# Recurrence and soft mixture of experts on one core: more unread matmuls around the first units, one gate in two halves, constants copied earlier, slot inputs in another PSUM bank

## The chip, the cores and the metric

The kernel runs on one core of one Trainium2 chip. The metric is device time in microseconds (us) of one execution; the time of a kernel is the median of its runs. The core has five instruction streams that run beside each other: TensorE (PE, with its weight loads as PEld), VectorE (DVE), ScalarE (ACT), GpSimd (POOL) and SyncE (SP, which here only issues transfers), and 16 transfer (DMA) engines that all queues share. TensorE writes to PSUM, which VectorE and ScalarE read; the other working memory is SBUF.

## The reference

Two layers follow each other. With x and f_logit of shape (4, 5056, 256), the first is a recurrence over the sequence, in each of the 4 sequences and 256 channels:

```python
f = lower_bound + (1.0 - lower_bound) * sigmoid(f_logit)
for t in range(S):
    h = f[:, t] * h + (1.0 - f[:, t]) * x[:, t]
    y[:, t] = h
```

The second is a soft mixture of experts over all N = 20224 tokens, with 8 experts of 4 slots each (32 slots) and a hidden width of 1024:

```python
logits = x @ phi                                   # N x 32
d = softmax of logits over the tokens              # to the slots
slot_input = d.T @ x                               # 32 x 256
slot_out[e] = relu(slot_input[e] @ w1[e]) @ w2[e]  # per expert
c = softmax of logits over the slots               # back to the tokens
return c @ slot_out                                # N x 256
```

The slots need every token, so no row of the output can be made before the whole input has been read.

## The kernel before, in words

**Units.** The 5056 tokens of a sequence are cut into 10 groups of 512 (the last two are shorter or overlap). One group of one sequence is a *unit*: 40 units, numbered 0 to 39. Units 0 to 3 are loaded one at a time; from unit 4 on (`long`) two neighbouring groups of one sequence are loaded as a pair, 1 MB of f_logit and 1 MB of x, by SyncE (`load`, lines 207 to 224). The tiles of the loads have three buffers each, so a load waits until the gate (f_logit) or the product (x) of the pair three before it is done.

**What one unit goes through**, each step on its own engine:

- `gate` (226): ScalarE takes the sigmoid of -f_logit, which gives s = 1 - sigmoid. It works on one unit (k=1) or on a pair (k=2, the default).
- `enter` (236): GpSimd multiplies s by x and gives u (unit 0: VectorE).
- `s_to_channels` (266) and `u_to_channels` (275): TensorE transposes s and u to put channels on partitions. Units 0 to 3 take four 128x128 transposes; a long unit takes, for u, eight half transposes (`half_to_channels`, 260), the first four from the u of the pair's even unit and the last four from that of the odd one. So a long unit's u needs the products of both units of its pair.
- `decay` (288): ScalarE turns the transposed s into the factor of the recurrence.
- `scan` (323, instruction at line 332): VectorE runs the recurrence, two scans of 512 tokens for a unit.
- `to_tokens` (339) and `keep_tokens` (355): TensorE transposes the states back, and VectorE or ScalarE copies them out of PSUM. There is one PSUM buffer for this.
- For each two groups: `logits` (371), `exps` (383), `weights_to_tokens` (390) and `slots` (423), which adds to the slot inputs in `slot_ps`.

**Order.** The order of the instructions on each engine is written out by hand: a prologue for units 0 to 2 (lines 481 to 498), then a loop over n from 0 to 39 (499 to 595), in which step n starts the scan of unit n, the u of unit n+1, the s of units n+2 and n+3, the product of unit n+3 and the loads six units ahead. `SINGLE` is 4, so `n < SINGLE - 2` are steps 0 and 1. Each engine works off its own list in order.

**Unread matmuls.** `idle` (177) issues f32 matmuls of 128x256 whose sum nobody reads, into the second half of the bank that holds `slot_ps`; the moving operand is `wide_rep`, a view of the constant `rep`. Its first call opens that half with two small bf16 matmuls (`first=True`). The kernel before calls it first at step 2, and then at steps 9, 13, 14, 15 and so on, behind the u of unit n+1.

**Constants.** `rep` holds the 32x32 identity repeated; GpSimd copies it out of an identity in four parts, one for each sequence (`rep_constants`, 84), two in step 0 and two in step 1, each behind the product of the step (`enter`).

**Weights.** GpSimd also issues the loads of the experts' weights (`load_w`, 135), which are read as f32 and stored as bf16, at steps 9, 17, 25, 31 to 34 and 36; the last matrix comes in three parts, and the last two go into a tile `w_t` that reuses a buffer of f_logit.

**The end.** After the last unit come the slot inputs. `slot_sb` is copied out of `slot_ps`; two small products per half put channels on partitions in `sin_ps` (616), a part of the bank `tail[:, 0]`, which also takes the row sums (`row_sums`, 407; at 621 and 622 they follow directly). Lines 631 and 632 read `sin_ps`, on VectorE and on ScalarE. Then come the hidden layer (638 to 656), the second layer (681 to 706, products at 696) and `slot_out` (708). From 713 on the output: matmuls with the tokens' weights (727, 760, 801), division by the row sums on VectorE and ScalarE, and stores issued by SyncE.

Of the kernel before, what the change touches and what calls it, by code (L numbers as in the profile page):

```python
# [18 lines left out]
def kernel(  # L19
# [10 lines left out]
    nc = tc.nc  # L30
# [73 lines left out]
    def lb_constants():  # L104
        row = lb_row.rearrange("u (p o) -> u p o", o=DC)
        lb_ps = ptp.tile([P, R, P], F32, name="lb_ps", tag="tp")
        lb = lb_ps[:, 0, ds(0, DC)]
        for o in range(DC):
            nc.tensor.transpose(lb_ps[:, 0, ds(o, 1)], row[:, :, o], ident_f[ds(0, 1), ds(0, 1)])
        nc.vector.tensor_scalar(omlb, lb, -1.0, 1.0, ALU.mult, ALU.add)  # L110
        nc.vector.tensor_scalar(nomlb, lb, 1.0, -1.0, ALU.mult, ALU.add)
# [50 lines left out]
    with tc.tile_pool(name="sp2", bufs=3) as sp2, \  # L162
# [11 lines left out]

        wide_rep = rep.rearrange("p b s -> p (b s)").unsqueeze(1).broadcast_to([P, 2, P])

        def idle(k, first=False):
            if first:
                for i in range(2):
                    nc.tensor.matmul(slot_bank[:, 1, ds(0, P)], ident, ident,  # L180
                                     start=True, stop=False, skip_group_check=True)
            for _ in range(k):
                nc.tensor.matmul(slot_bank[:, 1], ident_f, wide_rep,  # L183
                                 start=False, stop=False, skip_group_check=True)
        xs, fs, sts, uts, pss, psus, hs, hps, hts, lgs, ets = ({} for _ in range(11))

# [39 lines left out]
        def gate(n, k=2):  # L226
            if n % 2 == 0:
                sts[n // 2] = sp2.tile([P, 2, R, D], BF16, name="s_t", tag="s_t")
            s_t, f_t = sts[n // 2][:, ds(n % 2, k)], fs[n // 2][:, ds(n % 2, k)]
            if n // B == odd:  # L230
                m = R7 * D
                s_t = s_t.rearrange("p u r d -> p (u r d)")[:, :m]
                f_t = f_t.rearrange("p u r d -> p (u r d)")[:, :m]
            nc.scalar.activation(s_t, f_t, ACT.Sigmoid, scale=-1.0)  # L234
# [22 lines left out]
                nc.tensor.matmul(v[:, :, :, r], t(r)[k].bitcast(F32), sides,  # L257
                                 is_transpose=True, start=True, stop=True)

        def half_to_channels(n, ps, t):  # L260
            k = ds(n % 2 * (P // 2), P // 2)
            v = ps.rearrange("c p r -> c (p r)").rearrange("c (p r) -> c p r", r=2 * R)
            for r in range(2 * R):
                nc.tensor.transpose(v[:, :, r], t(r)[k].bitcast(F32), ident_f[k, k])  # L264

        def s_to_channels(n):
            if n % 2 == 0:
                pss[n // 2] = psp.tile([P, 2, P, R], F32, name="sp", tag="sp")
            ps = pss[n // 2][:, n % 2]
            if n // B == odd:  # L270
                woven_to_channels(n, ps, lambda r: sts[n // 2][:, r // R, r % R])
            else:
                to_channels(n, ps, sts[n // 2][:, n % 2])

        def u_to_channels(n):
            ps = psu.tile([P, P, R], F32, name="up", tag="up")
            if long(n):
                half_to_channels(n, ps, lambda r: uts[n - n % 2 + r // R][:, r % R])
            elif n // B == odd:
                woven_to_channels(n, ps, lambda r: uts[n - n % 2 + r // R][:, r % R])  # L280
            else:
                to_channels(n, ps, uts[n])
            psus[n] = ps.rearrange("c p r -> c (p r)").bitcast(BF16).rearrange(
                "c (t o) -> c t o", o=DC)
# [149 lines left out]
        def unit(f, m):  # L434
            if 0 <= m < n_unit:
                f(m)
# [45 lines left out]
            load(n, 1)  # L482
        load(SINGLE)
        lb_constants()
        gate(0, 1)
        enter(0)
        s_to_channels(0)
        decay(0, 1, [0])
        u_to_channels(0)
        gate(1, 1)  # L490
        decay(0, 1, [1])
        phi_constants()
        enter(1)
        s_to_channels(1)
        u_to_channels(1)
        gate(2, 1)
        decay(1, 1)
        enter(2)
        for n in range(n_unit):
            if n < SINGLE - 2:  # L500
                if n:
                    unit(to_tokens, n - 1)
                    unit(u_to_channels, n + 1)
                s_to_channels(n + 2)
                if n + 3 < SINGLE:
                    gate(n + 3, 1)
                decay(n + 2, 1)
                if n + 3 == SINGLE:
                    gate(n + 3)
                if n % 2 == 0:  # L510
                    unit(load, n + AHEAD)
                unit(enter, n + 3)
                for b in range(2 * n, 2 * n + 2):
                    rep_constants(b)
            else:
                end = n >= n_unit - 6
                if n % 2 == 0:
                    unit(load, n + AHEAD)
                    if n == SINGLE - 2:
                        to_tokens(n - 1)  # L520
                        keep_tokens(n - 1)
                    if not end and n >= SETTLED:
                        unit(gate, n + 4)
                else:
                    unit(decay, n + 1)
                    if n in (late + 1, late + 3):
                        keep_tokens(n - 2)
                    if n < SETTLED:
                        gate(n + 3)
                    if n == n_unit - 5:  # L530
                        gate(n + 3)
                        exps(odd - 1)
                if not end and n != n_unit - 7:
                    group(exps, n - 2)

                unit(enter, n + 3)
                for _ in range(W_AT.get(n, 0)):
                    load_w(w_next[0])
                    w_next[0] += 1

                if n in (n_unit - 3, n_unit - 2):
                    unit(u_to_channels, n + 1)
                if n in (late, late + 2):
                    to_tokens(n - 2)
                elif n not in (SINGLE - 2, late - 1, late + 1):
                    unit(to_tokens, n - 1)
                if n == n_unit - 2:
                    keep_tokens(n - 1)
                if n % 2 == 0:
                    unit(s_to_channels, n + 2)  # L550
                    unit(s_to_channels, n + 3)
                if n not in (n_unit - 3, n_unit - 2):
                    unit(u_to_channels, n + 1)
                if n in (n_unit - 5, n_unit - 4):
                    idle(2)
                elif n == SINGLE - 2:
                    idle(1, True)
                elif 2 * B <= n < n_unit - 4 and n % (2 * B) in (1, 5, 6, 7):
                    idle(1)
                if n == n_unit - 2:  # L560
                    tail = psp.tile([P, 2, G], F32, name="tail", tag="sp")
                    sums = tail[:, 0]
                    rs_ps = sums[:, ds(0, n_grp * R * B)].rearrange(
                        "p (q b) -> p q b", b=B)
                    late_ps, odd_ps = (
                        tail[:, 1].bitcast(BF16)[:, ds(i * R * P, R * P)].rearrange(
                            "p (r s) -> p r s", r=R) for i in range(2))
                    logits(odd)
                    exps(odd)
                    slots(odd - 2)  # L570
                elif not end and by_pairs(n - 1):
                    if n % B == 0:
                        g = (n - 1) // (2 * B) * 2
                        for i in range(2):
                            logits(g + i, [2, 3] if n % (2 * B) == 0 else [0, 1])
                elif not end:
                    group(logits, n - 1)
            if n == n_unit - 1:
                odd_weights()
                logits(last, [0, 1, 2])  # L580

            unit(scan, n)
            if n in (late, late + 2):
                keep_tokens(n - 2)
                to_tokens(n - 1)
            elif n not in (SINGLE - 2, late - 1, late + 1, n_unit - 2):
                unit(keep_tokens, n - 1)
            if n == n_unit - 3:
                weights_to_tokens(odd - 1, nc.scalar.copy)
            elif not n >= n_unit - 6:  # L590
                group(weights_to_tokens, n - 3)
                batch(slots, n - 4, 0)
                batch(slots, n - 4, 1)
                if n > 2 * B and n % (2 * B) == 3:
                    idle(1)
# [17 lines left out]
        slot_sb = hpool.tile([P, G, DC], BF16, name="slot_sb", tag="h")  # L613
        slot_sb = slot_sb.rearrange("p t o -> p (t o)").bitcast(F32)[:, ds(0, D)]
        nc.vector.tensor_copy(slot_sb, slot_ps)
        sin_ps = tail[:, 0, ds(G // 2, DC * NS)].rearrange("p (o s) -> p o s", o=DC)
        slot_v = slot_sb.rearrange("p (c o) -> p o c", o=DC)
        for o in range(DC):
            nc.tensor.matmul(sin_ps[:, o], slot_v[:, o], rep[:, 0],
# [250 lines left out]
```

## Time and profile before

| what | value |
|---|---|
| time, median of 3 runs | 197.94 us (197.11, 197.94, 198.4) |
| the profiled execution | 197.01 us, its span 195.2 us |
| mean granted TensorE clock | 0.845 |
| PE busy, share of the span | 150.6 us, 77% |
| DVE | 142.0 us, 73% |
| ACT | 138.8 us, 71% |
| POOL | 103.1 us, 53% |
| read from HBM, written to it | 58.23 MB, 20.71 MB |

The span runs from the first to the last instruction of the profiled execution; 1.8 us of its time lie outside. Times in a view are counted from the start of the span. The page gives busy time by engine, the span in 40 slices, the chain of waits that ended last and the costliest groups of instructions; the trace behind it also answers with a timeline of any stretch and with tables of stretches. A group's line reads: line of the kernel, engine, operation, output<-inputs, shapes, count | busy us, mean ns of one | idle time of the engine just before them, and what ended it:

```profile
L245 POOL TENSOR_TENSOR u_t<-s_t,x_t 128x1024 bf16<-128x1024 bf16 (+1 forms) x39 | 82.4, 2129 | 24.5 <-ACT s_t L234 14.2
L332 DVE TENSOR_TENSOR_SCAN h<-a,h,up 128x512 bf16<-128x512 f32 x64 | 78.1, 1267 | 9.0 <-PE up L264 4.3
...
L183 PE MATMUL slot_ps<-rep,ident_f 128*128 128x256 f32 x42 | 14.2, 426 | 0.0
```

The product of one unit takes GpSimd 2.13 us and one scan takes VectorE 1.27 us, two for a unit; the 21 unread matmuls show as 42 records, two for each f32 matmul. Busy time on TensorE is modelled, since its matmuls overlap.

### The profile page before, as it was taken

Reading aid. Unit: us, or ns where it says so; the run is one execution under the profiler, and the core shown is the slowest. Engines: PE = TensorE matmul, PEld = TensorE weight load, DVE = VectorE, ACT = ScalarE, POOL = GpSimd, SP = SyncE. Lnnn points to the kernel's source line nnn. Section 1 sums busy time; section 2 is a strip of 40 time slices with the busy share of each in tenths; the row PEclk is TensorE's granted clock in tenths of the full one; section 3 lists DMA queues with packets and bytes.
Section 4 is the critical chain, followed back from the end, with each engine's and each line's share of the span. In section 5 each row is a group of like instructions: output and inputs, shape, how many; then the busy total and the mean of one; then the engine's idle time right before and its main releaser. Section 6 shows DMA issues by size and latency. Waiting matters only on the chain.

```text
span 195.2 us, 3283 instructions
## 1 busy us (share of the span) xinstructions
PE 150.6 (77%) x1222; PEld 108.7 (56%) x1222; DVE 142.0 (73%) x175; ACT 138.8 (71%) x192; POOL 103.1 (53%) x78
## 2 busy tenths in 40 slices
PE   0684896898998979989798976999997999980000
PEld 0474775765786657857576755766872663420000
DVE  2666699799699999999999999824288867770000
ACT  3686778599988998989988698724068788991000
POOL 2584888756798949776888979592030000000000
PEclk9998799699699999999999999999985555555555
DMA  6999999999999999999999999999949999999995
GB/s 203 415 433 428 426 425 421 430 426 411 326 428 426 423 334 405 423 425 414 324 418 418 235 212 214 214 212 211 170 165 428 425 431 426 430 433 430 430 430 218
DMA packets 12145, 70.75 MB, mean 362 GB/s; under 512 B 1361, under 2 KB 1874, under 8 KB 7650
## 3 DMA queue, kind: packets, MB, share of 16 engines
q1 hardware_dynamic: 9504, 62.13, 76.3%
q0 software_dynamic: 2624, 8.42, 21.8%
q8 instruction: 9, 0.15, 0.3%
q14 instruction: 6, 0.05, 0.1%
q10 hardware_dynamic: 2, 0.00, 0.0%
HBM read 58.23 MB, written 20.71 MB: 404 GB/s over the span
## 4 chain that ended last, share of the span: by engine, by line
PE 36%; DVE 28%; DMA 17%; ACT 4%; issue 4%; SPq 1%; POOL 0%; ACTq 0%
DVE h L332 17%; DMA w_t<-in_moe_w_dram 7%; PE op L801 7%; PE sp L249 7%; PE op L727 6%; DMA w_sb<-in_moe_w_dram 6%; PE hp L345 5%; DVE ht L364 5%; PE up L264 4%; DMA f_t<-in_f_logit_dram 4%; DVE h L319 3%; DVE oc L717 2%; PE op L760 2%; ACT s_t L234 1%; PE lg L378 1%
## 5 line engine op out<-in xcount | busy, mean ns | idle before, releaser
L245 POOL TENSOR_TENSOR u_t<-s_t,x_t 128x1024 bf16<-128x1024 bf16 (+1 forms) x39 | 82.4, 2129 | 24.5 <-ACT s_t L234 14.2
L332 DVE TENSOR_TENSOR_SCAN h<-a,h,up 128x512 bf16<-128x512 f32 x64 | 78.1, 1267 | 9.0 <-PE up L264 4.3
L234 ACT ACTIVATE s_t<-f_t 128x2048 bf16<-128x2048 f32 (+2 forms) x22 | 38.1, 1736 | 2.9 <-DMA f_t<-in_f_logit_dram 2.9
L345 PE MATMUL hp<-ident_f,h 128*128 128x128 f32 (+1 forms) x160 | 29.3, 307 | 8.4 <-DVE ht L364 6.3
L297 ACT ACTIVATE a<-sp,lbs 128x1024 f32<-128x1024 bf16 x28 | 29.6, 1112 | 4.6 <-PE sp L249 4.5
L345 PEld LDWEIGHTS hp<-ident_f,h 128*128 128x128 f32 (+1 forms) x160 | 23.2, 206 | 17.0 <-DVE ht L364 11.5
L249 PE MATMUL sp<-ident_f,s_t 128*128 128x128 f32 x144 | 23.7, 315 | 7.0 <-ACT s_t L234 5.7
L249 PEld LDWEIGHTS sp<-ident_f,s_t 128*128 128x128 f32 x144 | 19.6, 164 | 8.7 <-ACT s_t L234 6.5
L264 PE MATMUL up<-ident_f,u_t 64*128 64x64 f32 x224 | 21.4, 236 | 2.4 <-POOL u_t L245 2.4
L264 PEld LDWEIGHTS up<-ident_f,u_t 64*128 64x128 f32 x224 | 17.0, 144 | 7.1 <-POOL u_t L245 2.8
L721 ACT ACTIVATE ob<-op,rrow 128x256 f32<-128x256 f32 x32 | 12.4, 478 | 9.1 <-PE op L727 8.7
L364 ACT COPY ht<-hp 128x512 f32<-128x512 f32 (+1 forms) x21 | 12.2, 583 | 7.9 <-PE hp L345 7.9
L304 ACT ACTIVATE a<-sp,lbs 128x512 f32<-128x512 bf16 (+2 forms) x16 | 13.2, 868 | 2.9 <-PE sp L249 2.7
L183 PE MATMUL slot_ps<-rep,ident_f 128*128 128x256 f32 x42 | 14.2, 426 | 0.0
L364 DVE COPY ht<-hp 128x512 f32<-128x512 f32 (+1 forms) x19 | 12.7, 668 | 1.0 <-PE hp L345 1.0
L801 PE MATMUL op<-slot_bd,etall 64*128 64x512 bf16 x32 | 13.1, 627 | 0.0
L812 ACT ACTIVATE oc<-op,rrow 128x256 f32<-128x256 f32 x32 | 12.2, 486 | 0.8 <-PE op L801 0.3
L727 PE MATMUL op<-slot_out,etall 32*128 32x256 bf16 x64 | 12.6, 375 | 0.1
L806 DVE TENSOR_TENSOR oc<-op,rrow 128x1024 f32<-128x1024 f32 x8 | 9.7, 1223 | 3.4 <-PE op L801 3.4
L717 DVE TENSOR_TENSOR ob<-op,rrow 128x1024 f32<-128x1024 f32 (+2 forms) x12 | 9.8, 862 | 2.2 <-DMA out_dram<-ob 1.1
L727 PEld LDWEIGHTS <-etall 32*128 32x128 bf16 x64 | 8.9, 153 | 3.8 <-issue 1.3
L378 PE MATMUL lg<-h,phi 128*32 128x512 bf16 (+1 forms) x80 | 9.9, 389 | 0.2 <-ACT et L402 0.2
(109 smaller groups left out, 168.9 us busy)
## 6 DMA issues: line engine op xcount, KB each, us to landing
f_t<-in_f_logit_dram SPq DMA_DIRECT2D x14, 1024.0 KB, 11.2
x_t<-in_x_dram SPq DMA_DIRECT2D x14, 1024.0 KB, 9.5
out_dram<-oc SPq DMA_DIRECT2D x4, 2048.0 KB, 13.1
w_sb<-in_moe_w_dram POOLq DMA_DIRECT2D x14, 512.0 KB, 9.5
out_dram<-ob SPq DMA_DIRECT2D x3, 2048.0 KB, 9.6
f_t<-in_f_logit_dram SPq DMA_DIRECT2D x8, 512.0 KB, 7.0
x_t<-in_x_dram SPq DMA_DIRECT2D x8, 512.0 KB, 6.1
out_dram<-oc SPq DMA_DIRECT2D x4, 896.0 KB, 6.0
```

The lines of the kernel that those rows point to most:

```text
L183: nc.tensor.matmul(slot_bank[:, 1], ident_f, wide_rep, start=False, stop=False, skip_group_check=True)
L234: nc.scalar.activation(s_t, f_t, ACT.Sigmoid, scale=-1.0)
L245: nc.gpsimd.tensor_tensor(uts[n][:, :r], s_t[:, :r], x_t[:, :r], ALU.mult)
L249: nc.tensor.transpose(ps[:, :, r], t[:, r].bitcast(F32), ident_f)
L264: nc.tensor.transpose(v[:, :, r], t(r)[k].bitcast(F32), ident_f[k, k])
L297: nc.scalar.activation(a, sp[:, :, :, :, o], ACT.Identity, scale=nomlb[:, ds(o, 1)], bias=1.0)
L332: nc.vector.tensor_tensor_scan(h[:, :T, o], decays[n // 2, o][:, n % 2, :T], up[:, :T, o], hs[number(g - 1, b)][:, ds(used(g - 1) - 1, 1), ...
L345: nc.tensor.transpose(hp[:n_p, r], hw[:, :n_p, r], ident_f)
L364: copy(hts[g][:n_p, b].rearrange("p r d -> p (r d)").bitcast(F32), hps.pop(n)[:n_p].rearrange("p r c -> p (r c)"))
L717: nc.vector.tensor_tensor(ob, op, scale.broadcast_to(list(ob.shape)), ALU.mult)
L727: nc.tensor.matmul(op[:, j], ew[:, :, r + j], slot_out[ds(b * NS, NS)], start=True, stop=True, skip_group_check=True)
L801: nc.tensor.matmul(op[:, i_r].rearrange("p u d -> p (u d)"), ew[:, :, r + i_r], slot_bd[ds(j * 2 * NS, 2 * NS)].rearrange("s u d -> s (u d)"),
```

## The change

- `idle` can take another moving operand. `plain`, a view of the identity, is there from the start, while `rep` is not.
- New calls: three in front of unit 0's s (with the opening that step 2 had), two in front of unit 1's s, one in front of unit 1's u, four at step 2 in front of the s of units 4 and 5, and one each at steps 3, 5 and 7 behind the u of unit n+1; at step 11, two in the middle of unit 12's u, between its two halves. In all 15 more.
- The gate of units 4 and 5, at step 1, is issued as two instructions of one unit each.
- In step 1 the last two copies of `rep` come in front of unit 4's product on GpSimd, no longer behind it. With the two of step 0 all four now stand between the products of units 3 and 4.
- `sin_ps` moves from the bank of the row sums to the half bank that `idle` writes.

```diff
+        plain = ident_f.unsqueeze(1).broadcast_to([P, 2, P])
+
-        def idle(k, first=False):
+        def idle(k, first=False, moving=wide_rep):
             if first:
                 for i in range(2):
                     nc.tensor.matmul(slot_bank[:, 1, ds(0, P)], ident, ident,
                                      start=True, stop=False, skip_group_check=True)
             for _ in range(k):
-                nc.tensor.matmul(slot_bank[:, 1], ident_f, wide_rep,
+                nc.tensor.matmul(slot_bank[:, 1], ident_f, moving,
                                  start=False, stop=False, skip_group_check=True)
...
-        def half_to_channels(n, ps, t):
+        def half_to_channels(n, ps, t, rests=False):
...
             for r in range(2 * R):
+                if r == R and rests:
+                    idle(2)
                 nc.tensor.transpose(v[:, :, r], t(r)[k].bitcast(F32), ident_f[k, k])
...
             if long(n):
-                half_to_channels(n, ps, lambda r: uts[n - n % 2 + r // R][:, r % R])
+                half_to_channels(n, ps, lambda r: uts[n - n % 2 + r // R][:, r % R],
+                                 n == 3 * B)
...
         lb_constants()
+        idle(3, True, plain)
         gate(0, 1)
         enter(0)
         s_to_channels(0)
         decay(0, 1, [0])
         u_to_channels(0)
+        idle(2, moving=plain)
         gate(1, 1)
         decay(0, 1, [1])
         phi_constants()
         enter(1)
         s_to_channels(1)
+        idle(1, moving=plain)
         u_to_channels(1)
...
                 if n + 3 == SINGLE:
-                    gate(n + 3)
+                    gate(n + 3, 1)
+                    gate(n + 4, 1)
                 if n % 2 == 0:
                     unit(load, n + AHEAD)
-                unit(enter, n + 3)
+                if n == 0:
+                    unit(enter, n + 3)
                 for b in range(2 * n, 2 * n + 2):
                     rep_constants(b)
+                if n:
+                    unit(enter, n + 3)
...
+                if n == SINGLE - 2:
+                    idle(4, moving=plain)
                 if n % 2 == 0:
                     unit(s_to_channels, n + 2)
                     unit(s_to_channels, n + 3)
...
-                elif n == SINGLE - 2:
-                    idle(1, True)
+                elif n in (SINGLE - 2, SINGLE - 1, SINGLE + 1, SINGLE + 3):
+                    idle(1)
...
-        sin_ps = tail[:, 0, ds(G // 2, DC * NS)].rearrange("p (o s) -> p o s", o=DC)
+        sin_ps = slot_bank[:, 1, ds(0, DC * NS)].rearrange("p (o s) -> p o s", o=DC)
```

## The prediction

> **What bounds the kernel now.** I read the slices of the span first, then the chain that ended last, then the end of the input stage as a timeline, then tables of stretches. The three rows of slices (the granted TensorE clock, the busy share of the transfer engines, what they moved):
>
> ```profile
> PEclk9998799699699999999999999999985555555555
> DMA  6999999999999999999999999999949999999995
> GB/s 203 415 433 428 426 425 421 430 426 411 326 428 426 423 334 405 423 425 414 324 418 418 235 212 214 214 212 211 170 165 428 425 431 426 430 433 430 430 430 218
> ```
>
> One slice is 4.88 us. The transfer engines are full in every slice but the first, the one at 146 us and the last. From slice 22 on GB/s halves with the share unchanged: the weights are then read as f32 and stored as bf16, so 212 stored is 424 read. The page gives 58.23 MB read; at the 427 that the stretch from 10 to 20 us shows that takes 136.4 us, and the stream in fact runs from about 2.6 to 141.5 us, 138.9 us. The clock row has three dents, at slices 3-4, 7 and 10. The chain that ended last, near the end of that stream (start, length, what):
>
> ```profile
> 126.92 14.59 DMA w_t<-in_moe_w_dram
> 141.52 0.04 issue
> 141.56 0.39 PE so_ps L696 x2
> 141.95 0.02 issue
> 141.98 0.49 DVE slot_out L708
> ```
>
> The last weights were issued at 126.92, landed at 141.52 behind everything queued before them, and the output waits for them. The timeline of TensorE shows how nearly the arithmetic was late too:
>
> ```profile
> 139.50 1.79 PE L696 MATMUL so_ps<-w_t,wide 128*128 128x256 bf16 x14
> ...
> 141.56 0.38 PE L696 MATMUL so_ps<-w_t,wide 128*128 128x256 bf16 x2 [0.27 <-DMA w_t<-in_moe_w_dram]
> ```
>
> TensorE came to the last two products 0.27 us before their weights. So two chains end together: arithmetic at 141.29 and the load stream at 141.52. The change shortens only the first. Where it has room, the timeline of VectorE, which paces units 2 to 39, shows; in brackets the idle time before the group and what ended it:
>
> ```profile
> 21.44 2.46 DVE L332 TENSOR_TENSOR_SCAN h<-a,h,up 128x512 bf16<-128x512 f32 x2 [2.63 <-PE up L249]
> ...
> 39.11 2.45 DVE L332 TENSOR_TENSOR_SCAN h<-a,h,up 128x512 bf16<-128x512 f32 x2 [1.51 <-PE up L264]
> ...
> 52.80 2.45 DVE L332 TENSOR_TENSOR_SCAN h<-a,h,up 128x512 bf16<-128x512 f32 x2 [1.61 <-PE up L264]
> ```
>
> Each of the three waits lies in a dent. Stretches cut where the clock changes (length, busy time of PE, PEld, DVE, ACT, POOL with counts, clock, transfer share, GB/s):
>
> ```profile
> 15.11:18.52 3.41, 0.73 (x6) 0.54 (x5) 2.65 (x3) 3.06 (x3) 0.95 (x3) 1.00 1.00 423
> 18.52:21.94 3.42, 3.42 (x15) 3.17 (x16) 0.79 (x2) 1.42 (x2) 3.16 (x4) 0.50 1.02 434
> ...
> 32.18:35.59 3.41, 1.85 (x14) 1.49 (x15) 3.38 (x4) 3.36 (x3) 2.25 (x2) 1.00 1.01 425
> ...
> 45.83:49.24 3.41, 2.44 (x30) 1.62 (x30) 3.41 (x5) 3.38 (x3) 1.22 (x1) 1.00 1.03 390
> ...
> 69.72:73.14 3.42, 2.45 (x30) 1.65 (x30) 3.42 (x5) 3.42 (x4) 2.26 (x2) 1.00 1.04 313
> ```
>
> After a stretch of 3.41 us in which TensorE was busy for 0.73, 1.85 or 2.44 us, the next one was granted half the clock; after one of 2.45 (69.72) it was not.
>
> **The change, part by part.** *Gate in two halves.* One activation of 1.91 us becomes two of 1.06 (the row of units 0 to 3), 0.21 us more ScalarE. Unit 4's half is done at 16.56 + 1.06 = 17.62 instead of 18.47, unit 5's at 18.68; SyncE's next f_logit load, which waits for both, goes out 0.2 later into a full queue. Unit 5's four transposes then end near 19.3 at full clock (eight take 1.04 at 24.99, 1.97 at half clock), unit 3's four (0.63) at 19.95, and the scan that began at 21.44 begins near 19.97. *Constants.* Two copies (0.61 us) move ahead of unit 4's product into GpSimd's wait of 2.48 us there. Queued behind them are that product and unit 5's; unit 4's x lands at 5.61 + 12.6 = 18.2 (its issue and its time to landing), so the product starts at 18.2 in place of 18.60 and unit 5's ends at 18.2 + 2 x 2.14 = 22.5 in place of 23.64. No DMA is issued by GpSimd in this stretch; SyncE's load that waits for this product goes out a microsecond earlier, into a full queue. Unit 4's scan needs that product's transposes (0.47): 23.0 instead of 24.39. Gain on VectorE's chain 1.4 us.
>
> *Unread matmuls.* Fifteen more of 128x256 in f32, two records each; one at 55.46 let the next transpose start at 56.00, so 0.54 each. They go into TensorE's waits: 1.96 us before unit 0 (two small ones, 0.42, and three: 2.0), 1.19 before unit 1's s (two: 1.1), 0.57 before its u (one), 2.68 before unit 4 (four: 2.2, but that wait is now 0.85 shorter, so 0.3 over), 0.37, 0.61 and 0.36 before the transposes behind units 3, 5 and 7 (one each: 0.17 and 0.18 over, one hidden), 0.82 between the halves of unit 12 (two: 0.26 over). Queued behind each are the next transposes, and VectorE's scan waits for those: at most 0.9 us in all if every cover is gone. If they do keep the clock, the waits of 1.51 and 1.61 us go, 3.1 us, since the eight transposes there fall from 1.92-1.97 to 1.04. No row shows an unread matmul in these places: their worth lies between 0 (dents stay) and 3.1; I take 3.1, as the dented stretches were idle for 2.7, 1.6 and 1.0 us and the added work fills most of that.
>
> *Slot inputs in their own bank.* The two conversions of the slot input waited for the row sums that follow it in the old bank: 131.21, though its own matmuls ended at 129.85 + 0.61 = 130.46. VectorE's can start there; TensorE, behind row sums to 131.10, begins the hidden layer near 131.1 in place of 131.52. Gain 0.4.
>
> Sum for the arithmetic: 1.4 + 3.1 + 0.4 - 0.9 = 4.0 us earlier. What is late next is the stream: TensorE now waits for the last weights, and the end moves only with their landing. The stream is full and the order of its issues is the same, so a lead in arithmetic buys transfer time only where the engines were short of work. That is 106 to 112 us, where the weights begin to be issued: 195 GB/s stored in 110 to 112 (390 read), against 427, loses 0.17 us, and about as much before it. Bounds 0 and 0.4; I take 0.2. Against its own execution (197.01, span 195.2 and 1.8 around it) the sum is 196.8. The median of the three runs, 197.94, stands 0.93 above that execution. If their excess is late arithmetic (dents in other places; the slack is only 0.27 us), it goes; if it is the stream's rate, it stays. I take nearly half of it: 196.8 + 0.4 = 197.2.
>
> **The rivals.** *A: the stream sets the end* (above): 196.4 to 197.9. For it: share 1.0 throughout, loads landing 6 to 16 us after issue.
>
> *B: the dents stay or move.* Rows for: 2.44 and 2.45 us of busy time with different outcomes, so where a window is cut decides. Against: the added work raises the busy time of all three stretches. Price: no 3.1, perhaps the 0.9 of added work, less 1.4 + 0.4 gained: arithmetic still 0.9 us earlier, so nothing is lost, and part of the excess goes: 197.3 to 197.9; with the 1.4 lost as well, 0.5 us later against 0.27 of slack: 198.2. The Trainium skill ("TensorE: Matmul & The Clock Gate", Part 1, What's actually happening) says that the clock's windows run free of the kernel's start; by it every execution cuts its dents elsewhere, and the nearly equal pair of rows agrees. The same page (Why this matters for your kernels) asks for idle gaps of about 3 us before the clock falls; the trace disagrees, since the longest idle gap ahead of the dents is 2.68 us and ahead of the third 0.82.
>
> *C: slower, by the clock at the output's start.* The last full weights of the second matrix but two land at 122.51 + 14.0 = 136.5, and their eight products take 1.03: 137.5. What is left lands at 138.9, 140.2, 140.9 and 141.5 (issues plus 15.9, 16.7, 16.4, 14.6) and takes 1.8 us. So with a lead of 4 us TensorE idles for 2.2 of the last 4.0 us, where the stretch from 137.99 to 141.40 is now busy for 3.30 of 3.41; about 1.6 would be left, less than the 1.85 after which the clock was halved. The half clock then meets the last two products (0.38), and the first two matmuls of the output, and delays all the output, as the stream of stores is full behind it: +0.4 to 0.6 us; the pieces after that are paced by the conversions (0.48 each), not by TensorE. With no excess removed that is 197.94 + 0.5 = 198.5, slower than before. It decides from a lead of about 2 us on and if a window is cut there. Against: the stretch from 114.10 to 117.51, busy for 2.30 with 0.9 us of unread matmuls among it, was not followed by a dent, and the last products are matmuls of the same full width.
>
> *D: the stream itself gets faster.* Deeper queues could lift it to the 429 GB/s of the store stage's slices: 58.23 / 429 = 135.7 us, 3.2 us less, 193.8. Against: share is 1.0 already with queues 7 to 12 us deep. The Trainium skill ("DMA: Bandwidth & Descriptors", Where 436 GB/s comes from) sets the ceiling at 435 GB/s, by which 133.9 us would do, 5 us less; the trace touches 435 only in the stores, 156 to 176 us.
>
> **How the numbers follow.** A 0.66, B 0.13, C 0.13, D 0.07, and 0.01 for none of them. The time is A's, 197.2. The range takes A whole, B, and C to its price: 196.0 to 198.5; D is left out. A measurement of this kernel tells about 1%, 2 us. Faster by that (under 195.96) is D: 0.07. Slower by that (over 199.9) would be C at four times its price; of C and the unnamed I put 0.03 there. Within 1%: 0.90.
>
> **What would show it.** Clock row without dents in slices 3 to 10; the three waits of VectorE near 0; VectorE's last scan ends before 123 (now 125.6); TensorE's waits for the last weights grow from 0.27 to over 1.5 us in sum; the last weights still land between 141 and 141.6. I am wrong if they land before 140, or if TensorE again comes to the last products within 0.3 us of them.

## The result, and the profile after

| | before | after |
|---|---|---|
| time, median (runs) | 197.53 us (6, 196.81 to 198.5) | 200.05 us (6, 199.28 to 201.29) |
| the profiled execution, its span | 197.01, 195.2 us | 199.28, 197.5 us |
| instructions of TensorE in the trace | 2480 | 2540 |

Both were timed side by side. The ratio is 1.0137, with a 95% interval of 1.0093 to 1.0181: 2.5 us slower, where 197.2 us was forecast. Medians here and below are over all runs, while the ratios leave out executions that count as slow, so the two can differ. The profiled executions lie 2.27 us apart, and those can be taken to pieces. The slices of the span after (4.94 us each):

```profile
PEclk9999999699999999999999999999785555555555
DMA  6999999999999999999999999999559999999992
GB/s 211 420 433 428 426 421 425 425 428 366 369 426 426 396 346 426 426 426 332 399 414 376 236 216 211 213 212 213 86 197 433 421 438 421 418 438 448 438 425 123
```

Of the three dents in the clock row one is left, at slice 7. But where the input ends (slices 28 and 29) the transfer engines now stand at 5 tenths twice, where before one slice stood at 4. The timeline of VectorE, after (idle time before the group in brackets):

```profile
19.18 2.46 DVE L337 TENSOR_TENSOR_SCAN h<-a,h,up 128x512 bf16<-128x512 f32 x2 [0.98 <-PE up L251]
23.00 2.33 DVE L337 TENSOR_TENSOR_SCAN h<-a,up 128x512 bf16<-128x512 f32 x2 [0.78 <-PE up L268]
...
38.18 2.45 DVE L337 TENSOR_TENSOR_SCAN h<-a,h,up 128x512 bf16<-128x512 f32 x2 [1.61 <-PE up L268]
50.59 2.45 DVE L337 TENSOR_TENSOR_SCAN h<-a,h,up 128x512 bf16<-128x512 f32 x2 [0.34 <-PE up L268]
...
128.75 0.25 DVE L645 TENSOR_SCALAR sin<-slot_ps,lbs 128x32 bf16<-128x32 f32 x1 [0.86 <-PE slot_ps L633]
...
143.04 0.48 DVE L722 TENSOR_SCALAR slot_out<-so_ps,rcs 128x256 bf16<-128x256 f32 x1 [5.88 <-PE so_ps L710]
```

The arithmetic did get its lead: the slot input is converted at 128.75 instead of 131.21, 2.46 us earlier. `slot_out` nevertheless starts at 143.04, not at 141.98. The timeline of TensorE between the two:

```profile
136.39 1.03 PE L710 MATMUL so_ps<-w_sb,wide 128*128 128x256 bf16 x8
139.90 3.11 PE L710 MATMUL so_ps<-w_t,wide 128*128 128x256 bf16 x16 [2.47 <-DMA w_t<-in_moe_w_dram]
142.80 1.06 PE L152 MATMUL tail<-w_sb 128*128 128x128 bf16 x8
143.92 1.90 PE L741 MATMUL op<-slot_out,etall 32*128 32x256 bf16 x16
```

TensorE waits 2.47 us for the first part of the last weights, then runs the last 16 products in 3.11 us, because the clock was halved: the stretches of the clock say why (columns as in the tables above, the clock third from the end).

```profile
136.96:140.37 3.41, 0.94 (x10) 0.69 (x8) 0.20 (x2) 0.00 (x0) 0.00 (x0) 1.00 1.01 184
140.37:143.78 3.41, 3.41 (x22) 2.52 (x19) 0.48 (x1) 0.00 (x0) 0.07 (x1) 0.51 0.12 19
```

After a stretch with 0.94 us of work the next one ran at 0.51. (Line 152 is eight unread matmuls that both kernels have behind the products; at half clock they take 1.06 us, not 0.61, and the output's first matmul stands behind them until 143.92, though `slot_out` ended at 143.53.) The difference of the spans, stage by stage, from the starts, ends and landings in the two traces:

| stage | before | after | later by |
|---|---|---|---|
| last weights land | 141.52 | 142.28 | 0.76 |
| from there to the start of `slot_out` | 0.46 | 0.76 | 0.30 |
| end of `slot_out` to the first store's issue | 1.12 | 1.39 | 0.27 |
| first store's issue to the last landing | 50.44 | 51.38 | 0.94 |

The sum is 2.27. The 0.57 in the middle is the half clock (rival C). The first and the last row, 1.70 us, were in no case of the prediction. The table of transfer queues over the time of the stores (143 to 198 us; packets, MB, share) differs in one line. Before:

```profile
q1 hardware_dynamic: 2592, 20.71, 89.1%
q14 instruction: 1, 0.01, 0.1%
```

After:

```profile
q1 hardware_dynamic: 2592, 20.71, 89.2%
q8 instruction: 1, 0.02, 0.1%
q14 instruction: 1, 0.01, 0.0%
```

The same bytes are stored, and one packet more goes over the engines: a block of instructions. The trace's list of transfers has each of them: 16384 bytes, 0.88 to 0.98 us on one of the 16 engines, nine in the whole span before, ten after. The tenth went out at 168.47, in the middle of the stores. The ninth went out at 141.24 before, when nearly all weights had landed, and at 137.70 after, when they had not. The trace has 16 landings for each load, one for each engine as it is read here. From that point on the last of them falls behind the others (times from the list of landings, us):

| part of the last matrix | before: last landing but one, last | after: last landing but one, last |
|---|---|---|
| 1 | 138.91, 138.92 | 138.76, 139.85 |
| 2 | 140.13, 140.24 | 140.02, 141.05 |
| 3 | 140.81, 140.87 | 140.70, 141.67 |
| 4 | 141.48, 141.52 | 141.33, 142.28 |

The last landing but one is 0.11 to 0.15 us earlier than before, and one is about a microsecond behind it in all four parts. (That the late one is the same engine each time is a reading too: the list doesn't name the engine.) The end of the stores looks the same. Counted from the first store's issue, the last two landings of all come at 50.06 and 50.44 us before, and at 50.43 and 51.38 us after. That gave the theory for the experiments: **the added matmuls cost by being fetched**. The 15 of them are 60 instructions (each f32 matmul of this kernel is two weight loads and two matmuls). TensorE's fetches move forward by that much, one of them lands in front of the last weights, and one more falls among the stores. The rivals: the **lead** itself does the harm (TensorE idle, half clock, other order of transfers), or the **other edits** do.

A rule bears on this that the prediction had not weighed. The Trainium skill ("Runtime: NRT & Kernel Launch", Instruction fetch mechanics) says that instructions are refilled in 16 KiB blocks of 256 over a transfer queue of the engine's own, and that the cost of a block's boundary is mostly hidden. Block size and queue agree with the 16384-byte packets here; that they are hidden does not, with 0.94 us in the stores.

### The profile page after: what moved, and what is told of

The parts are those of the page before. It is cut to its first block, busy times and chain, and to the rows that moved or that the text cites. A ratio compares the mean times of both kernels' runs of the same rounds, so it can differ in the third digit from the quotient of the medians.

```text
span 197.5 us, 3344 instructions
## 1 busy us (share of the span) xinstructions
PE 154.7 (78%) x1252; PEld 111.3 (56%) x1252; DVE 142.3 (72%) x175; ACT 139.1 (70%) x193; POOL 103.2 (52%) x78
## 4 chain that ended last, share of the span: by engine, by line
PE 28%; DMA 21%; DVE 19%; ACT 8%; POOL 8%; issue 4%; SPq 2%; ACTq 0%; POOLq 0%
DVE h L337 12%; DMA x_t<-in_x_dram 11%; DMA w_t<-in_moe_w_dram 9%; PE op L815 7%; POOL u_t L247 6%; PE op L741 6%; PE up L268 4%; PE hp L350 3%; PE sp L251 3%; DVE ht L369 3%; DVE h L324 3%; ACT oc L781 2%; ACT s_t L236 2%; POOL w_sb L147 2%; PE so_ps L710 2%
## 5 line engine op out<-in xcount | busy, mean ns | idle before, releaser
L350 PE MATMUL hp<-ident_f,h 128*128 128x128 f32 (+1 forms) x160 | 28.5, 301 | 7.1 <-DVE ht L369 5.1
L251 PE MATMUL sp<-ident_f,s_t 128*128 128x128 f32 x144 | 20.9, 288 | 3.0 <-ACT a L309 1.4
L251 PEld LDWEIGHTS sp<-ident_f,s_t 128*128 128x128 f32 x144 | 17.4, 149 | 5.3 <-ACT s_t L236 2.8
L185 PE MATMUL slot_ps<-rep,ident_f 128*128 128x256 f32 x52 | 17.1, 419 | 0.0
L337 DVE TENSOR_TENSOR_SCAN h<-a,up 128x512 bf16<-128x512 f32 x8 | 9.4, 1210 | 1.7 <-PE up L268 0.8
```

The lines of the kernel that those rows point to most:

```text
L185: nc.tensor.matmul(slot_bank[:, 1], ident_f, moving, start=False, stop=False, skip_group_check=True)
L251: nc.tensor.transpose(ps[:, :, r], t[:, r].bitcast(F32), ident_f)
L337: nc.vector.tensor_tensor_scan(h[:, :T, o], decays[n // 2, o][:, n % 2, :T], up[:, :T, o], hs[number(g - 1, b)][:, ds(used(g - 1) - 1, 1), ...
L350: nc.tensor.transpose(hp[:n_p, r], hw[:, :n_p, r], ident_f)
```

## The experiments

The fetches and stages of all kernels, each from its profiled execution (us; instructions of TensorE as the trace records them; the stage of the stores is from the first store's issue to the last landing; the last column is the median against that of the kernel before in the same session):

| kernel | instr. | 9th fetch | 10th fetch | last weights land | stores | median |
|---|---|---|---|---|---|---|
| before | 2480 | 141.24 | none | 141.52 | 50.44 | |
| after | 2540 | 137.70 | 168.47 | 142.28 | 51.38 | +2.5 |
| e1_tail_count | 2540 | 141.60 | 178.87 | 141.74 | 51.40 | +1.0 |
| e2_no_added | 2480 | 141.38 | none | 141.62 | 50.43 | 0.0 |
| e3_no_spin | 2524 | 137.74 | 173.26 | 142.32 | 52.73 | +2.3 |
| e4_fill_wait | 2539 | 138.20 | 167.72 | 142.15 | 51.41 | +1.8 |
| e5_front_count | 2540 | 139.44 | 167.93 | 142.29 | 51.40 | +1.9 |
| e6_same_count | 2480 | 143.47 | none | 143.49 | 50.42 | +3.1 |
| e7_matmuls_only | 2540 | 138.72 | 168.17 | 142.52 | 51.42 | +2.2 |
| e8_front_20 | 2500 | 141.19 | none | 141.65 | 50.44 | +0.3 |
| e9_front_40 | 2520 | 141.86 | 173.41 | 143.56 | 51.38 | +1.9 |

The expectations of e1 to e4 count from the 197.5 us of the first six runs; in their own session the kernel before took 197.10.

**e1_tail_count: the count alone, at the end.** The kernel before, with 30 unread bf16 matmuls (60 instructions) behind TensorE's last work, where nothing waits for them:

```diff
                 couple(i, j)
+        extra = pout.tile([P, R, D], F32, name="op", tag="op")
+        for _ in range(30):
+            nc.tensor.matmul(extra[:, 0, ds(0, P)], ident, ident,
+                             start=True, stop=True, skip_group_check=True)
```

> The kernel before, with 30 unread bf16 matmuls (60 instructions) behind the last matmul of TensorE, where nothing waits for them. Instruction theory: TensorE's instructions come in transfers of 16 KB, one for some 256 of them, and each holds one of the 16 transfer engines for 0.95 us; the longer program needs a tenth one, in the middle of the stores, so the last store lands about 0.9 us later and the first store is issued when it was (143.6): 197.5 becomes 198.4. Clock theory (the half clock at the start of the output is the whole of the loss): nothing changes here, 197.5, and stores take 50.4 us from the first issue to the last landing.

Measured: 198.13 us against 197.10, ratio 1.0052 (1.0017 to 1.0087). Its queues over the stores:

```profile
q1 hardware_dynamic: 2592, 20.71, 89.2%
q8 instruction: 1, 0.02, 0.1%
q14 instruction: 1, 0.01, 0.1%
```

Up to the first store nothing moved by more than 0.23 us, and the stage of the stores takes 51.40 us, 0.96 more. Matmuls that do nothing and for which nobody waits cost the time of one fetch.

**e2_no_added: the change without the 15 matmuls.** Gate in halves, constants, slot inputs in their own bank stay.

```diff
         lb_constants()
-        idle(3, True, plain)
         gate(0, 1)
...
-                elif n in (SINGLE - 2, SINGLE - 1, SINGLE + 1, SINGLE + 3):
-                    idle(1)
+                elif n == SINGLE - 2:
+                    idle(1, True)
```

(and so at the other new calls)

> The changed kernel without the fifteen added unread matmuls: gate in halves, constants and slot inputs stay as changed. The program is as long as before. Instruction theory: nine transfers of instructions, none in the stores, and the last weights land near 141.4 again; arithmetic is 0.5 to 2 us ahead, so 197.0 to 197.8, not slower than before. Theory that the lead itself costs (arithmetic ahead, TensorE idle before the last weights, half clock): 198 to 198.5 if the lead exceeds 2 us, with a half-clock stretch that begins between 138 and 144.

Measured: 197.13 us, ratio 0.9990 (0.9965 to 1.0015), twelve runs within 196.90 and 197.49. The timeline of its TensorE:

```profile
139.07 1.03 PE L703 MATMUL so_ps<-w_t,wide 128*128 128x256 bf16 x8 [1.38 <-DMA w_t<-in_moe_w_dram]
140.33 1.09 PE L703 MATMUL so_ps<-w_t,wide 128*128 128x256 bf16 x6 [0.22 <-DMA w_t<-in_moe_w_dram]
141.67 0.38 PE L703 MATMUL so_ps<-w_t,wide 128*128 128x256 bf16 x2 [0.25 <-DMA w_t<-in_moe_w_dram]
```

The slot input is converted at 129.12, 2.1 us earlier than in the kernel before, and most of that turns into waits for the last weights (1.85 us in sum, where the kernel before had 0.27). No half clock follows here. So this lead neither gains nor costs, and the three edits other than the matmuls are free.

**e3_no_spin and e4_fill_wait: the half clock.** Both are the changed kernel. e3 drops the eight unread matmuls behind the last products; e4 moves them into the wait in front of those, and makes them longer.

```diff
-        spin(tail[:, 1], 8, P)
```

```diff
         for j in range(Q):
+            if j == 2:
+                spin(tail[:, 1], 8, 4 * P)
             for fc in range(FC):
...
-        spin(tail[:, 1], 8, P)
```

> The changed kernel without the eight unread matmuls that stand between the last product and the output. At half clock they take 1.06 us and the first output matmul starts 0.40 us after its operand is ready. Both theories: that 0.36 us goes, 199.7. If only their sixteen instructions matter (the tenth transfer of instructions falls away): 1.2 us less, 198.9.

> The changed kernel with those eight unread matmuls moved: 512 columns wide, in front of the first product that waits for the last weights, so that TensorE is busy for 1.7 of the 2.5 us of that wait. As many instructions as the changed kernel. Clock theory: no half clock at 140 to 144, the loss goes entirely, 197.5. Instruction theory: full clock saves 0.6 to 0.7 us between the landing of the last weights and the first store, and the last weights still land near 142.3 and a tenth transfer of instructions still falls into the stores: 199.3 to 199.5.

Measured: e3 199.38 us, ratio 1.0106 (1.0052 to 1.0159); e4 198.89, ratio 1.0077 (1.0053 to 1.0101). TensorE in e4:

```profile
137.99 1.89 PE L152 MATMUL tail<-w_sb 128*128 128x512 bf16 x7
140.28 1.69 PE L712 MATMUL so_ps<-w_t,wide 128*128 128x256 bf16 x14 [0.41 <-DMA w_t<-in_moe_w_dram]
142.19 0.38 PE L712 MATMUL so_ps<-w_t,wide 128*128 128x256 bf16 x2 [0.22 <-DMA w_t<-in_moe_w_dram]
```

With the wait filled the last two products take 0.38 us as before, the clock is not halved between 38 and 147 us, and of the 1.8 us that remain the late weights and the tenth fetch make 1.6: 0.63 + 0.97 by the table. So the half clock is worth some 0.6 to 0.7 of the 2.5 by the stages and the medians; the intervals of the two ratios (1.0093 to 1.0181, 1.0053 to 1.0101) overlap, and the ratios by themselves don't fix it.

e3's result is mixed. Sixteen instructions fewer did not save the tenth fetch (173.26), so its third case, 198.9, is out. Whether the expected 0.36 us went can't be told, as its interval overlaps that of the changed kernel. Its profiled execution (200.44 us, a microsecond above the median) had the half clock from 141 us to the end, and its table of stretches shows a cost of that which the changed kernel did not have:

```profile
148.00:150.00 2.00, 2.00 (x10) 0.71 (x9) 1.68 (x3) 1.97 (x6) 0.00 (x0) 0.50 0.98 406
150.00:152.00 2.00, 1.51 (x5) 0.31 (x2) 1.84 (x4) 2.00 (x7) 0.00 (x0) 0.50 0.52 217
```

The transfer share falls to 0.52 in the midst of the first stores. The output pieces come later: the first of the stores of `oc` goes out 6.28 us after the first store, where the changed kernel needed 4.38. The stage of the stores takes 52.73 us there. That the half clock alone makes the pieces late is likely, but no run sets it apart.

**e5_front_count and e7_matmuls_only: the matmuls alone.** Both are the kernel before. e5 puts 30 tiny bf16 matmuls (60 instructions) into TensorE's first wait, 0.98 us of work far ahead of the last weights; e7 has the change's own 15 matmuls at their places and none of its other edits.

```diff
         lb_constants()
+        for i in range(30):
+            nc.tensor.matmul(slot_bank[:, 1, ds(0, NS)], ident, ident[:, ds(0, NS)],
+                             start=True, stop=False, skip_group_check=True)
         gate(0, 1)
```

> The kernel before, with 30 very short unread bf16 matmuls (60 instructions, 32 columns each) in TensorE's first wait, in front of unit 0: as many instructions as the changed kernel, all ahead of the last weights, but no lead in arithmetic and no other change. Instruction theory: every transfer of instructions comes 60 instructions earlier, so the ninth falls before the last weights have landed (137.5 to 139.5 instead of 141.2) and they land near 142.2; a tenth falls into the stores; about 0.7 + 0.95 us more: 198.6 to 198.9. Theory that the lead or the half clock costs: 197.1, like before.

> The kernel before with the fifteen added unread matmuls alone: gate of units 4 and 5 in one, constants and slot inputs as before. Instruction theory: nearly the whole loss is here, ten transfers of instructions, one in the stores, the last weights near 142.2: 198.7 without a half clock at the start of the output, up to 200.5 with it. If gate, constants or the bank of the slot inputs had a part in the loss: under 198.2.

Measured: e5 199.06 us against 197.20, ratio 1.0084 (1.0056 to 1.0113), a little above what was expected; e7 199.43, ratio 1.0115 (1.0061 to 1.0169), within it. In e5 the slot input is converted at 130.98, as late as before, and still TensorE stands waiting in front of the second half of the last products:

```profile
139.26 1.04 PE L699 MATMUL so_ps<-w_t,wide 128*128 128x256 bf16 x8
141.53 1.19 PE L699 MATMUL so_ps<-w_t,wide 128*128 128x256 bf16 x8 [1.23 <-DMA w_t<-in_moe_w_dram]
```

Its ninth fetch went out at 139.44; the last landing but one of the second part of the last matrix then came at 140.24, and the last at 141.48. So the count costs without any lead, and (e2) the lead costs nothing without the count. e7 loses 1.00 us up to the last weights and 0.98 in the stores, with no half clock between 38 and 147 us: the whole of its 2.0 us of span.

**e6_same_count: the changed kernel with as many instructions as before.** Twenty of the later unread matmuls and six of the new ones in f32 (four instructions each) become bf16 ones of the same shape (two each).

```diff
+        def brief(k):
+            for _ in range(k):
+                nc.tensor.matmul(slot_bank[:, 1], ident, small,
+                                 start=False, stop=False, skip_group_check=True)
...
                 elif 2 * B <= n < n_unit - 4 and n % (2 * B) in (1, 5, 6, 7):
-                    idle(1)
+                    brief(1)
```

(and the like at the other calls; the eight at the end become four long ones in the wait, as in e4)

> The changed kernel with all its unread matmuls in place, but with as many instructions as before: six of those in front and the twenty from step 9 on are bf16 (two instructions each instead of four), and the eight before the output are four of 512 columns in the wait for the last weights. Instruction theory: nine transfers of instructions, the ninth at 141 or later, the last weights near 141.5, no transfer in the stores: 196.9 to 197.4. Theory that a lead of 2 us or the unread matmuls themselves cost: 198.5 or more, as in the run with the filled wait (198.89).

Measured: 200.25 us, ratio 1.0082 (1.0037 to 1.0127). A miss as to the sum. The part on the stores held: nine fetches, none among the stores, stage 50.42. But the clock row:

```profile
PEclk9999789999996999999995599699995555555555
```

The bf16 matmuls take less of TensorE's time (0.28 us at full clock, where an f32 pair shows 0.70), the clock was halved at 60 us, from 104.6 to 114.8 and at 125 us, and the arithmetic came late: the slot input at 134.04, `slot_out` at 145.32. The profiled execution thus doesn't decide between the theories; it suggests that the twenty later f32 ones earn their 80 instructions. Its twelve runs spread from 197.43 to 201.48 us, and the mean granted clock goes with them: 0.846 and 0.851 in the two shortest (197.43 and 197.66), 0.824 in the profiled one. The two with the higher clock came out close to the 196.9 to 197.4 that the instruction theory gives, but no trace of them is there to show why.

**e8_front_20 and e9_front_40: how much is too much.** As e5, with 10 and with 20 tiny matmuls (`range(10)`, `range(20)`): 20 and 40 instructions.

> The kernel before with ten very short unread matmuls in TensorE's first wait, 20 instructions instead of the 60 of the run before. Instruction theory: the cost comes in steps, one for each transfer that is moved or added. In the runs so far the tenth transfer came when some 2500 instructions were done, and this program has 2500, the one before 2480: so no tenth transfer, stores 50.4 us from the first issue to the last landing. The ninth comes 20 instructions earlier, about 139.5 to 140.5, still ahead of the last weights: they land near 142.2, 197.8 to 198.0. A cost in proportion to the instructions would give 197.7, with a third of each of the two steps; no cost of instructions, 197.1.

> The same with twenty of them, 40 instructions. Instruction theory in steps: 2520 instructions, so the tenth transfer is there and the stores take 51.4 us, and the last weights land near 142.2, as with 60: 198.7 to 199.0. In proportion: 198.3.

Measured: e8 197.33 us against 197.04, ratio 1.0024 (0.9985 to 1.0063); e9 198.95, ratio 1.0096 (1.0073 to 1.0118). In the stage of the stores the cost comes in a step, not by the instruction: 50.44 us with twenty, 51.38 with forty. Twenty cost nothing clear of the noise, against an expectation of 197.8 to 198.0 (the interval of e8's ratio alone would also allow a cost in proportion): no tenth fetch, and the ninth stayed at 141.19, where it had been expected a microsecond or two earlier. Forty bring the tenth. The counts fit one boundary: where the tenth went out, TensorE had started 2499 to 2537 of the recorded instructions (in all seven kernels that have one), and the kernels that end at 2480 or 2500 never fetched it. In e9 the delay before the stores arose elsewhere than in e5, since its ninth fetch did not come earlier (141.86). Its TensorE:

```profile
141.05 1.03 PE L699 MATMUL so_ps<-w_t,wide 128*128 128x256 bf16 x8 [0.85 <-DMA w_t<-in_moe_w_dram]
142.35 1.01 PE L699 MATMUL so_ps<-w_t,wide 128*128 128x256 bf16 x6 [0.26 <-DMA w_t<-in_moe_w_dram]
143.60 0.38 PE L699 MATMUL so_ps<-w_t,wide 128*128 128x256 bf16 x2 [0.25 <-DMA w_t<-in_moe_w_dram]
```

All weights are late, the last by 2.04 us. Of that 0.84 us is the last landing but one (142.32 instead of 141.48): the stream was late as a whole, as a load that landed at 121.67 before landed at 122.69; what made it late was not followed up. The rest is one landing. The load ahead of the fetch at 123.02 ended 0.25 us after its last landing but one, the load behind it 1.33 us (124.97 and 126.30), and the last weights still 1.24 us. In the kernel before the fetches at 126.39 and 135.27 left no such trace. The list doesn't tell which of the 16 engines a fetch goes to, so why one fetch delays the last engine and another doesn't stays open. And this execution took 200.10 us, 1.15 above the median of its twelve: what the usual one loses ahead of the stores, about a microsecond, no trace shows.

## Why the prediction was wrong, step by step

**What held.** The load stream sets the end: e2 shows a lead of 2.1 us that moves nothing. The slot inputs in their own bank no longer wait for row sums (0.86 us on their own products alone). Gate and constants did what was worked out: unit 4's scan begins at 23.00 us, forecast 23.0, before 24.39; e2, without the added matmuls, has 23.23. The scan that waited 2.63 us at 21.44 begins at 19.18, and what unit 4's scan waits for next (0.78 us) is the transposes behind the two products of its pair, 18.13 to 22.37 us, 18.2 to 22.5 in the forecast.

**What looked right and isn't shown.** In the profiled execution after, the dents at slices 3-4 and 10 went, and the third wait fell from 1.61 to 0.34. But dents come and go without any change of code. e1 is the kernel before up to its last matmul, and it has no third dent and a third wait of 0.33; after, e3 and e4 are alike up to the last weights and have one, none and two dents. Where a window falls differs from execution to execution, as rival B said, so the dents that went can't be put down to the added matmuls. What is steady is another effect, which the prediction missed: the row of the clock shows full speed up to its first record, but four 128x128 transposes took 1.06 to 1.12 us until 15.11 before, and 0.63 right after; 1.06 is also what four took in the dent at 20.28. So TensorE had started at half clock. The first record of the full clock lies at 7.0 to 8.1 us in the four kernels with the f32 matmuls in front of the first units (after, e3, e4, e7), and at 15.1 to 17.6 in the seven others, also in e6, where the ones in front are bf16.

**What was too large.** The second dent stayed (1.61 us after 1.51), although its stretch has one unread matmul more; of the 3.1 us 1.17 came in this execution (1.27 at the third wait, -0.10 at the second), and by e1 that may be chance. The last scan ended at 123.79, not before 123, and the slot input had a lead of 2.46 us, not 4.0. None of this moved the time. (One reading under rival D was off: 435 GB/s shows not only in the stores, but also from 11.70 to 15.11 us.)

**The step that failed.** "The stream is full and the order of its issues is the same", with the unread matmuls priced only by TensorE's time, "at most 0.9 us in all if every cover is gone". The order of the loads is the same, but the instructions themselves come through the same 16 engines, and that cost was put at nothing. The page of the kernel before showed it, in its table of queues (packets, MB, share of 16 engines):

```profile
q8 instruction: 9, 0.15, 0.3%
```

0.3% of all engines' span looks like nothing: 0.003 x 16 x 195.2 = 9.4 us of engine time, about one us a packet. But a packet sits on one engine, and a load or a store is over when its slowest engine is through. The price is therefore not 1/16 of a microsecond but up to a whole one where a wait ends with the slowest engine: 0.76 us at the last weights (up to 1.00 in e7) and 0.94 in the stores. The forecast that the last weights "still land between 141 and 141.6" is where it shows (142.28); the conditions for being wrong named only an earlier landing or a late TensorE, and neither came.

**Rival C** had its place and its price right: 0.94 us of work in the stretch (1.6 worked out, since the lead was thought to bring less idle time and the weights to land earlier), then the half clock, then 0.30 + 0.27 = 0.57 us, forecast as 0.4 to 0.6. It was wrong to set it beside the main case as an alternative with 0.13: here it came on top of the two other losses. With C alone (0.57 us on top of 197.5) the time would have been in the range; with both fetches it was 1.5 us above it. By e5 and e7 the matmuls' count costs 1.9 to 2.2 us without C.

**The excess of the median.** Of the 0.93 us by which the median of three runs lay above the profiled one, nearly half (0.4) was expected to stay. Most of the excess was the small sample: over 29 and twice 23 runs the kernel before has medians of 197.04 to 197.20, and e2 with its lead has 197.13.

## What to carry to other kernels

Where the transfer engines are full, a table of queues must be read for instruction blocks too: count an engine's instructions in blocks of 256, find when each block is fetched, and ask what is waiting for the slowest transfer engine just then. Unread matmuls that hold the clock are not free when they fill a wait; they may be added up to the next block (here 20 instructions cost nothing clear of the noise, 40 cost 1.9 us), and an f32 one counts four. And one profiled execution doesn't show that a dent of the clock is gone for good: the same code had it in one execution and not in another. A lead won ahead of a transfer that sets the end is idle time in front of it, and may cost the clock that the work behind it needs.

## What the runs showed of the hardware

- TensorE's instructions came in packets of 16384 bytes, one for about 256 instructions (the first at some 220 recorded ones, the ninth at some 2250), 0.88 to 1.14 us each, most under 0.98; one more of them among the stores made that stage 50.42 to 50.44 us into 51.38 to 51.42 us, in four kernels without it and six with it (e3, with the half clock from 141 us on, took 52.73).
- The last of a load's 16 landings, once behind in a full stream, stayed behind: 1.09 us at 139.85 and 0.95 at 142.28 (after), 1.33 us at 126.30 and 1.24 at 143.56 (e9).
- Each f32 matmul showed as four instructions, two weight loads and two matmuls; a bf16 one as two (15 and 30 unread ones both added 60).
- With the half clock from 144.8 us on, 1.2 us behind the first store, the share of the transfers stayed at 1.03 from 146 to 156 us (before); with it from 141.3 us on it fell to 0.52 at 150 us (e3, one execution).
- The f32 matmuls in front of the first units brought the full clock at 7.0 to 8.1 us instead of 15.1 to 17.6; six bf16 ones of the same shape (e6) did not: 15.9.
- The granted clock of one and the same code differed between executions: no dent from 8 to 141 us in e3, one in after, two in e4.
